# Loads of two batches issued from ScalarE's queue, and an instruction order from a table with a rank for every operation

## The chip, the cores and the metric

The kernel runs on one core of a Trainium2 chip. The core has TensorE (PE: matrix products, with its weight loads as PEld), VectorE (DVE), ScalarE (ACT), GpSimd (POOL) and SyncE (SP), which here only issues DMAs. The metric is the device time of one execution in microseconds; the median of the runs counts.

## The reference

Inputs are q, k and v of 4 batches, 8 heads, 576 positions and 64 features in float32, a memory `M_prev` (64 x 64 for each batch and head) with its norm `z_prev`, a gate `beta` for each head, and two weight matrices in float64 that the kernel reads as pairs of 32-bit words.

```python
scores = scale * np.matmul(q, k.transpose(0, 1, 3, 2))      # causal mask, softmax over the row
local = np.matmul(a, v)
q_p = phi(q)                                                # phi(x) = elu(x) + 1
mem_out = einsum('bhsd,bhde->bhse', q_p, M_prev) / mem_norm
attn = g * mem_out + (1 - g) * local
x = attn.transpose(0, 2, 1, 3).reshape(2304, 512)
h = x @ w_in                                                # 512 -> 2048
y = (np.maximum(h, 0) + alpha * np.minimum(h, 0)) @ w_out   # 2048 -> 512
```

## The kernel before

Precise products are made of float16 halves: a float32 value is split into a high and a low float16 part, and three of the four products are summed. Rows of the attention are worked off in blocks of 128: four blocks of 128 for each batch, and the first 64 rows of all four batches together as a fifth group (`Z`). For each batch `b`, `load_batch` (line 630) brings q, k, v, `M_prev` and `z_prev` into SBUF; keys go into tile `kn` and values into `vn`, of which there is one each, so that batch `b+1` can be loaded only when batch `b` has been read for the last time. `prep_qk`, `prep_v` and `prep_phi` (lines 825 to 904) find scales and the memory's norm; `build_qk` and `build_v` (lines 951 and 969) make the float16 halves and turn queries and keys by DMA transposes. For each head and pair of blocks, `unit_scores` makes the scores `s`, a VectorE operation masks them and finds the row's extreme, and ScalarE takes the exponential `E`. `unit_probs` (line 1056) writes the probabilities `P` as two halves (ScalarE the high, VectorE the low one) and has them turned by a DMA transpose into `PT`. `pair_values` (line 1096) multiplies `PT` with the values in the PSUM tile `bank`, splits the result into `xn` and has it turned by a DMA transpose into `x`. `moe_in` (line 1210) multiplies `x` with the first weights into `h`, and `moe_out` (line 1250) the activated `gg` with the second weights into `y`.

All DMAs, loads, stores and transposes alike, are issued from SyncE (`Y`); ScalarE is `A`. `load` (line 668) issues one load and gives its phase a name: `L2k`, for instance, is a load of batch 2's keys.

No engine's order is the order of the text. Every operation is first recorded by `Work.add` (line 282) with its dependences, its price (`price`, line 330) and its phase. `Work.issue` (line 459) then ranks the operations and calls `lay` (line 389), a list scheduler: each engine takes, when it is free, the ready operation of the lowest rank, by priced times. The operations are emitted in the order of the starts that `lay` gives. In the kernel before, the ranks come from a backward pass over the dependences, to which `STAGES` (line 32) adds biases by phase and by phase and engine, in two stages with further forward and backward passes. The phase names that the prediction uses are these: L2k to L3v are the loads of keys and values of batches 2 and 3, P21 is `unit_probs` of batch 2 for blocks 1 and 2, and `n` and `N` are warm-up products of TensorE on a tile of ones, at the start of the program, that nothing reads. The tile `stv` holds maxima of the values, from which scales are made.

Of the kernel before, what the change touches and what calls it, by code (L numbers as in the profile page):

```python
# [20 lines left out]
WC = [1, 1, 1, 1, 1, 1, 1, 1, 1, 1, 1, 1, 1, 1, 0, 1]  # L21
XB = 3
# [9 lines left out]
STAGES = [  # L32
    (2, {
        "A0": 10.6, "A:DVE": 50.6, "BK0": 102.5, "BK:ACT": -27.7, "BK:PE": 3.4, "C0": -56.4, "C1": 22.3, "C2": 335.8,
        "C3": -920, "C:ACT": 1096.2, "C:DVE": -3.8, "C:PE": -943.6, "I": -699.2, "I:DVE": 79.2, "I:POOL": 497.7,
        "J:ACT": 470.6, "J:DVE": 108, "J:PE": -179.3, "K": 47.5, "K:POOL": 2.3, "L0K": -713.8, "L0K:DMA": 228.2,
# [6 lines left out]
        "LW:DMA": 605.3, "LZ": 27.3, "LZ:DMA": -1145.9, "Lz": 8.5, "Lz:DMA": -8.6, "N": 87.9, "N:PE": 292.5,  # L43
        "P01": 4, "P03": 3.7, "P11": 777.2, "P13": 823.4, "P21": 168.1, "P23": 236.6, "P31": -675.3, "P33": -247.2,
        "P:ACT": 988.7, "P:DMA": 668.5, "P:DVE": -882.6, "P:PE": -157.8, "S0": 4737.2, "S1": -1253, "S3": -2953.6,
        "S:ACT": -87.5, "S:DVE": 168.1, "V0": -874.8, "V:DVE": 211.2, "V:PE": -90.8, "a0": 5.7, "a1": 46.8,
        "a2": -161.5, "a3": 389.6, "a4": -42.9, "a:ACT": -265.2, "a:DVE": 239.4, "bk0": -173.5, "bk1": 344.8,
        "bk2": 244.5, "bk3": 3.1, "bk:ACT": -687.5, "bk:DMA": 246.9, "bk:DVE": 1380.7, "bk:PE": 100.3, "bv0": -0.7,
# [5 lines left out]
        "o31": 144.8, "o33": 10.1, "o:ACT": -779.8, "o:DMA": 580.1, "o:DVE": -613.6, "o:PE": 33.3, "oZ": 10.8,  # L54
# [5 lines left out]
        "v:DVE": 634.9, "v:PE": 331.4, "x0": -121.5, "x:ACT": 2.1, "x:DVE": 73.7, "y0_10": -412.5, "y0_11": -68.6,  # L60
        "y0_30": 187.3, "y0_31": 1834.4, "y1_10": -18.1, "y1_11": 103.3, "y1_30": -419.6, "y1_31": 103.8,
        "y2_10": 184.2, "y2_11": 220.2, "y2_30": -3073.8, "y2_31": -122.6, "y3_10": 764.1, "y3_11": 98,
        "y3_31": 447.3, "y4_11": -1599.1, "y:ACT": -1231.1, "y:DMA": 642.8, "y:DVE": -750.7, "y:PE": 1282.7,
    }),
# [4 lines left out]
        "C3:PE": -8.9, "C:ACT": 13.2, "C:DVE": 9.3, "C:PE": -17.2, "I": -57.9, "I:POOL": -8.6, "J:ACT": -18.7,  # L69
# [6 lines left out]
        "LW3": -8.7, "LW3:DMA": -22.1, "LW:DMA": -2.8, "LZ:DMA": -42.6, "Lz:DMA": -4.4, "N": 0.9, "N:PE": -13.7,  # L76
# [5 lines left out]
        "P33:DMA": -3.8, "P33:DVE": -7.4, "P33:POOL": -37, "P:ACT": 15, "P:DMA": -20.1, "P:DVE": 8.9, "P:PE": -86.4,  # L82
# [126 lines left out]
        "y:PE": 143.8,  # L209
    }),  # L210
]
WINDOW = 3413.0
RING, SHARE = 1200, 0.95
NEG = -1.0e37
# [35 lines left out]
class Work:  # L250
# [31 lines left out]
    def add(self, kind, engine, name, a, kw):  # L282
# [35 lines left out]
        if kind == "DMA":  # L318
            hold, move, late, packets = hold
        elif kind == "PE":  # L320
            late = ins[0].shape[0] / 128
            x = kw.get("lhsT")
# [1205 lines left out]
```

## Time and profile before

| | us |
|---|---|
| three runs | 563.78, 561.42, 562.34 |
| median | 562.34 |
| profiled execution, device time | 563.66 |
| its span from the first to the last instruction | 561.9 |
| TensorE busy in the span | 536.4 |
| VectorE busy | 450.9 |
| ScalarE busy | 376.7 |

The profile is of one execution. The times of the runs are device times; the span leaves out what lies around the program's first and last instruction, 1.76 us here. A window row gives busy times of the engines in one stretch; TensorE's clock in it is the share of full speed that was granted. The DMA share in it adds up the times of the packets over the 16 DMA engines.

### The profile page before, as it was taken

The page shows a single profiled execution, that of the slowest core. Times are in us where ns is not written, and L with a number is a line of the kernel's source. Part 1 is how long each engine was busy: PE and PEld are TensorE (multiplying, and loading weights), DVE is VectorE, ACT ScalarE, POOL GpSimd, SP SyncE. Part 2 cuts the span into 40 slices and gives each one's busy share as a digit, 9 for nine tenths or more (in the row PEclk, how much of TensorE's full clock was granted, in tenths as well). Part 3 has the DMA queues.
Part 4 walks back from the last instruction along what each step waited for, and adds up shares of the span by engine and source line. Part 5 has one row for each costly group of instructions (what it writes and reads, how often), then busy time and mean ns, then how long its engine had stood idle before and what let it go on. Part 6 is the DMA issues. An engine that isn't in the chain of part 4 may idle for free. (4 is left out here: it accounts for less than half of the span.)

```text
span 561.9 us, 11984 instructions
## 1 busy us (share of the span) xinstructions
PE 536.4 (95%) x4421; PEld 353.5 (63%) x4421; DVE 450.9 (80%) x1197; ACT 376.7 (67%) x790; POOL 82.8 (15%) x142
## 2 busy tenths in 40 slices
PE   9749999999999899999998999999999999999997
PEld 3448654556557566658555766578578765866663
DVE  4989999999999799999897999998679974233232
ACT  2568996778998369978785787796579873232222
POOL 3000510031220012221222110431112110000000
PEclk9869999999999999999998999999999999999999
DMA  8998595836359997579999816799446963000000
GB/s 283 239 353 202 155 238 173 244 94 153 89 127 184 214 231 170 101 140 210 194 201 198 175 34 146 160 232 178 58 118 111 167 138 88 12 11 2 37 1 37
DMA packets 226026, 82.84 MB, mean 147 GB/s; under 512 B 216224, under 2 KB 216240, under 8 KB 225968
## 3 DMA queue, kind: packets, MB, share of 16 engines
q1 hardware_dynamic: 225968, 82.09, 64.5%
q8 instruction: 34, 0.56, 0.4%
q14 instruction: 24, 0.20, 0.1%
HBM read 35.66 MB, written 5.77 MB: 74 GB/s over the span
## 5 line engine op out<-in xcount | busy, mean ns | idle before, releaser
L487 PE MATMUL h<-x,R 128*128 128x256 f16 x1536 | 246.7, 273 | 1.9 <-DMA x<-xn 1.4
L487 PE MATMUL y<-R,gg 128*128 128x512 f16 (+1 forms) x832 | 247.0, 399 | 0.8 <-ACT k L487 0.6
L487 PE MATMUL bank<-v,PT 128*128 128x64 f16 x1224 | 182.1, 193 | 5.3 <-DMA PT<-P 4.5
L487 PEld LDWEIGHTS <-R 128*128 128x128 f16 x1536 | 148.6, 98 | 36.9 <-issue 6.5
L487 PEld LDWEIGHTS <-gg 128*128 128x128 f16 x768 | 74.4, 98 | 78.3 <-DVE gg L487 1.8
L487 PEld LDWEIGHTS <-PT 128*128 128x128 f16 x1224 | 114.4, 98 | 13.6 <-DMA PT<-P 6.9
L487 POOL TENSOR_SCALAR E<-q,nrm,sm 128x64 f32<-128x64 f32 x112 | 67.9, 618 | 310.9 <-DVE sm L487 269.8
L487 ACT ACTIVATE E<-E,mx 128x320 f32<-128x320 f32 (+3 forms) x136 | 81.1, 602 | 21.5 <-DVE mx L487 17.4
L487 DVE SCALAR_TENSOR_TENSOR P<-E,mx,P 128x384 f16<-128x384 f32 (+2 forms) x112 | 75.3, 699 | 8.5 <-ACT P L487 8.4
L487 ACT ACTIVATE P<-E,mx 128x384 f16<-128x384 f32 (+2 forms) x112 | 71.0, 675 | 15.8 <-POOL E L487 12.0
L487 DVE SCALAR_TENSOR_TENSOR r<-r,oma,h 128x256 f32<-128x256 f32 x128 | 56.6, 475 | 20.2 <-ACT r L487 20.0
L487 DVE SCALAR_TENSOR_TENSOR gg<-r,gsc,gg 128x512 f16<-128x512 f32 x56 | 41.8, 748 | 36.5 <-ACT gg L487 35.0
L487 ACT ACTIVATE r<-h 128x512 f32<-128x512 f32 x72 | 42.3, 589 | 35.8 <-PE h L487 23.9
L487 ACT ACTIVATE gg<-r,gsc 128x512 f16<-128x512 f32 x56 | 40.1, 717 | 37.4 <-PE y L487 33.4
L487 DVE CUSTOM_DVE_ANT_0 E<-s,mask,pm 128x320 f32<-128x320 f32 (+2 forms) x96 | 56.9, 608 | 7.6 <-PE s L487 7.5
L487 PE MATMUL s<-k,qT 128*128 128x64 f16 (+5 forms) x136 | 37.9, 294 | 1.3 <-DMA k<-k 1.3
L487 PE MATMUL s<-k,qS 128*128 128x192 f16 (+4 forms) x120 | 34.0, 294 | 0.0
L487 PE MATMUL h<-R 128*128 128x256 f32 x128 | 32.7, 383 | 0.0
L487 PEld LDWEIGHTS h<-R 128*128 128x128 f32 x128 | 22.3, 192 | 6.6 <-issue 3.0
L487 ACT ACTIVATION_READ_ACCUMULATOR E<-E,mx 128x1 f32 x124 | 23.5, 189 | 0.0
L487 ACT ACTIVATE xn<-bank,xsc 128x256 f16<-128x256 f32 x28 | 12.9, 462 | 12.3 <-PE bank L487 12.3
L487 DVE SCALAR_TENSOR_TENSOR xn<-bank,xsc,xn 128x256 f16<-128x256 f32 x28 | 13.4, 480 | 9.4 <-ACT xn L487 9.4
(183 smaller groups left out, 636.7 us busy)
## 6 DMA issues: line engine op xcount, KB each, us to landing
q<-in_q_dram SPq DMA_DIRECT2D x16, 256.0 KB, 4.3
vn<-in_v_dram SPq DMA_DIRECT2D x16, 256.0 KB, 5.2
out_dram<-t SPq DMA_DIRECT2D x16, 256.0 KB, 2.4
kn<-in_moe_w_in_dram SPq DMA_DIRECT2D x6, 512.0 KB, 6.7
kn<-in_moe_w_out_dram SPq DMA_DIRECT2D x6, 512.0 KB, 5.3
kn<-in_k_dram SPq DMA_DIRECT2D x12, 256.0 KB, 4.0
qS<-qT SPq DMA_DIRECT2D x24, 128.0 KB, 2.6
R<-in_moe_w_in_dram SPq DMA_DIRECT2D x4, 512.0 KB, 5.6
```

The source lines that it names most:

```text
L487: fn(*a, **kw)
```

## The change

Two things are changed. First, the loads of four phases, the keys and values of batches 2 and 3, are issued from ScalarE and no more from SyncE; `price`, `add` and `lay` learn that a DMA can be an operation of ScalarE. Secondly, `STAGES` with its backward passes is gone. In its place stands `PLAN`, a table with one rank for every operation of the program, 6253 in all, kept as differences under phase and engine; `issue` reads it and calls `lay` once. The prices of DMAs that `lay` uses are changed too. What is computed, the tiles and the operations remain as they are.

```diff
+ASIDE = ('L2k', 'L2v', 'L3k', 'L3v')
...
-STAGES = [
...
+PLAN = {
...
+    "L2k:ACT": "1959 -434 -66 47 1055",
+    "L2q:DMA": "1008 914 40 667 -99",
+    "L2v:ACT": "1575 63 -516 1340 -1369 1354",
+    "L3k:ACT": "3852 -400 -817 341 -99",
...
+    "L3v:ACT": "2938 -323 93 992 -880 1001",
...
+    "P21:ACT": "2836 -135 2 -585 610 -580 120 -122 633 -763 1082 288 -696 739 -700 197",
...
-        if kind == "DMA":
+        if kind == "DMA" or name == "dma_start":
             hold, move, late, packets = hold
...
-                return (800 + 1.75 * kb if kb > 400 else 1130 + 0.6 * kb), 190 + 3.45 * kb, 1655, -1
+                return (800 + 1.75 * kb, 4.1 * kb, 1700, -1) if kb > 400 else (1130 + 0.6 * kb, 3.78 * kb, 1885, -1)
...
-            return 620, (273 if kb > 200 else 200) + 4.17 * kb, 2100, packets
+            return (600, 4.5 * kb, 2050, packets) if kb > 200 else (620, 6 * kb, 2090, packets)
...
                 free[x] = done = t + hold
+                if x == "ACT" and move and not back:
+                    wire = max(wire, t + 100) + move
+                    done = wire + late
...
-        for passes, bias in STAGES:
-            rank = [x + 1e3 * sum(bias.get(k, 0) for k in dict.fromkeys((
-                op[7], op[7].rstrip("0123456789_") + ":" + op[0], op[7] + ":" + op[0]))) for x, op in zip(rank, ops)]
-            for n in range(passes):
-                if n:
-                    back = self.lay(after, before, [-s - h for s, h in zip(start, hold)], True)
-                    rank = [-s - h for s, h in zip(back, hold)]
-                start = self.lay(before, after, rank)
-            rank = start
+        plan = {}
+        for x, steps in PLAN.items():
+            at, ranks = 0, []
+            for step, _, times in (y.partition("*") for y in steps.split()):
+                for _ in range(int(times or 1)):
+                    at += int(step)
+                    ranks.append(100.0 * at)
+            plan[x] = iter(ranks)
+        start = self.lay(before, after, [next(plan[f"{op[7]}:{op[0]}"]) for op in ops])
...
     def load(o, i, phase):
         work.phase = phase
-        Y.dma_start(out=o, in_=i)
+        (A if phase in ASIDE else Y).dma_start(out=o, in_=i)
```

## Rows read from the trace of the kernel before

**Rows 1.** The page: busy time of the engines; the DMA queue.

```profile
PE 536.4 (95%) x4421; PEld 353.5 (63%) x4421; DVE 450.9 (80%) x1197; ACT 376.7 (67%) x790; POOL 82.8 (15%) x142
...
q1 hardware_dynamic: 225968, 82.09, 64.5%
```

**Rows 2.** Busy time by stretch: start:end and length, engines, clock, DMA share, GB/s.

```profile
20.00:44.00 24.00, 13.95 (x101) 10.77 (x102) 22.17 (x83) 15.49 (x52) 0.00 (x0) 0.66 1.12 291
180.00:196.00 16.00, 13.68 (x98) 8.86 (x95) 13.24 (x30) 6.74 (x11) 0.00 (x0) 1.00 0.98 200
280.00:292.00 12.00, 10.66 (x93) 5.96 (x92) 11.96 (x41) 10.09 (x23) 1.88 (x3) 1.00 1.16 225
292.00:304.00 12.00, 9.35 (x116) 7.46 (x114) 9.10 (x27) 7.77 (x19) 4.69 (x8) 1.00 1.01 174
304.00:308.00 4.00, 4.00 (x16) 1.71 (x14) 2.83 (x11) 2.04 (x5) 0.00 (x0) 0.57 0.93 210
...
196.00:212.00 16.00, 16.00 (x110) 10.43 (x108) 15.89 (x46) 11.65 (x29) 2.62 (x5) 1.00 1.02 230
212.00:240.00 28.00, 27.23 (x264) 18.85 (x262) 26.78 (x88) 25.52 (x58) 5.73 (x12) 1.00 0.63 138
460.00:558.00 98.00, 98.00 (x749) 63.51 (x745) 32.64 (x64) 30.20 (x48) 0.77 (x2) 1.00 0.10 28
...
304.00:320.00 16.00, 16.00 (x121) 11.26 (x119) 13.57 (x38) 10.38 (x25) 2.07 (x4) 0.89 1.03 217
```

**Rows 3.** TensorE's waits over the run: us in total, times, longest us.

```profile
PE bank L487 <- DMA PT<-P: 4.5, 5, 2.7
PE bank L487 <- DVE stv L487: 3.5, 1, 3.5
PE h L487 <- DVE P L487: 2.8, 1, 2.8
...
PE h L487 <- DMA x<-xn: 1.4, 2, 1.2
PE s L487 <- DMA k<-k: 1.3, 2, 0.9
```

**Rows 4.** SyncE's timeline: start us, us, what is issued.

```profile
198.58 4.04 SPq L487 DMA_DIRECT2D vn<-in_v_dram  x4
...
208.79 2.40 SPq L487 DMA_DIRECT2D kn<-in_k_dram  x2
...
294.14 2.07 SPq L487 DMA_DIRECT2D kn<-in_k_dram  x2
296.32 4.16 SPq L487 DMA_TRANSPOSE PT<-P  x1
...
300.59 1.33 SPq L487 DMA_TRANSPOSE PT<-P  x1
...
317.77 0.62 SPq L487 DMA_DIRECT2D kn<-in_k_dram  x1
```

**Rows 5.** VectorE's timeline from 292 us: the low halves of P.

```profile
292.70 1.06 DVE L487 SCALAR_TENSOR_TENSOR P<-E,mx,P 128x384 f16<-128x384 f32 x2 [0.47 <-ACT P L487]
...
294.68 1.01 DVE L487 SCALAR_TENSOR_TENSOR P<-E,mx,P 128x384 f16<-128x384 f32 x2
```

**Rows 6.** Timeline of all engines at 302 us: idle time before, releaser.

```profile
302.77 0.20 PE L487 MATMUL bank<-v,PT 128*128 128x64 f16 x1 [2.65 <-DMA PT<-P]
...
302.83 0.62 ACT L487 ACTIVATE P<-E,mx 128x384 f16<-128x384 f32 x1 [2.40 <-DMA PT<-P]
```

**Rows 7.** Tiles kn and PT, issues on SyncE: ns min/median/max, first and last start.

```profile
L487 SPq DMA_DIRECT2D kn<-in_k_dram x15: 399/868/2191, 124.2 to 317.8; - x15
...
L487 SPq DMA_TRANSPOSE PT<-P x56: 1309/1926/4159, 117.3 to 464.7; - x56
```

**Rows 8.** VectorE's timeline from 31 us: maxima of queries and of values.

```profile
31.51 0.68 DVE L487 TENSOR_REDUCE stq<-q 128x1 f32<-128x512 f32 x1
...
32.25 1.21 DVE L487 TENSOR_REDUCE stv<-R 128x1 f32<-128x1024 f32 x1
```

More of the change, by code (lines that the diff above doesn't have):

```diff
@@ L29 @@
 PN = [1, 1, 1, 1, 1]
-STAGES = [
[L33 to L36, printed above, removed]
[6 rows of a table removed]
[L43 to L48, printed above, removed]
[5 rows of a table removed]
-        "o31": 144.8, "o33": 10.1, "o:ACT": -779.8, "o:DMA": 580.1, "o:DVE": -613.6, "o:PE": 33.3, "oZ": 10.8,
[5 rows of a table removed]
[L60 to L64, printed above, removed]
[4 rows of a table removed]
-        "C3:PE": -8.9, "C:ACT": 13.2, "C:DVE": 9.3, "C:PE": -17.2, "I": -57.9, "I:POOL": -8.6, "J:ACT": -18.7,
[6 rows of a table removed]
-        "LW3": -8.7, "LW3:DMA": -22.1, "LW:DMA": -2.8, "LZ:DMA": -42.6, "Lz:DMA": -4.4, "N": 0.9, "N:PE": -13.7,
[5 rows of a table removed]
-        "P33:DMA": -3.8, "P33:DVE": -7.4, "P33:POOL": -37, "P:ACT": 15, "P:DMA": -20.1, "P:DVE": 8.9, "P:PE": -86.4,
[21 rows of a table removed]
-        "h4_11:PE": -16.7, "h:ACT": 10, "h:DVE": 8.9, "h:PE": -16.3, "n": -27.5, "n:PE": -9.4, "o01": -15,
[5 rows of a table removed]
-        "o33:DVE": 21.3, "o33:PE": -55.2, "o:ACT": -0.5, "o:DMA": -50.1, "o:DVE": 13.1, "o:PE": -18, "oZ": -97,
[4 rows of a table removed]
-        "q:ACT": 39, "q:DVE": 9.7, "r0:ACT": 0.9, "r0:DVE": 9.9, "r:ACT": 35.7, "r:DVE": 13.6, "s01:ACT": -1.2,
[4 rows of a table removed]
-        "s33:ACT": 1.7, "s33:PE": -49.1, "s:ACT": 12.1, "s:DVE": 8.9, "s:PE": -16.3, "sZ": 8.1, "sZ:ACT": 98.3,
[14 rows of a table removed]
-        "y4_11:PE": -16, "y:ACT": 21.9, "y:DMA": 2.5, "y:DVE": 8.4, "y:PE": -16.3,
-    }),
[4 rows of a table removed]
-        "C3:PE": -26.7, "C:ACT": 47.4, "C:DVE": -22.5, "C:PE": 1, "I:DVE": -32.9, "I:POOL": 4.3, "J": 37.8,
[13 rows of a table removed]
-        "P33:DMA": -13.2, "P33:DVE": -9.1, "P:DMA": -3.5, "P:DVE": -22.3, "P:PE": 0.2, "P:POOL": -11, "S0": 2.9,
[27 rows of a table removed]
-        "o33:PE": 65.8, "o:ACT": 7.4, "o:DMA": -10.7, "o:DVE": -24.8, "o:PE": 144.2, "oZ": -53.6, "oZ:ACT": 8.9,
[9 rows of a table removed]
-        "s33:DVE": -8.2, "s33:PE": 41.6, "s:ACT": -5, "s:DVE": -22.3, "s:PE": 143.8, "sZ": -0.9, "sZ:ACT": 37.5,
[15 rows of a table removed]
-        "y:PE": 143.8,
-    }),
-]
@@ L212 @@
+PLAN = {
[440 rows of a table added]
+}
 WINDOW = 3413.0
@@ L335, in price @@
         size = 2 if o.dtype == F16 else 4
-        if kind == "DMA":
+        if kind == "DMA" or name == "dma_start":
             kb = n * o.shape[0] * size / 1024
             if "transpose" in name:
-                return (800 + 1.75 * kb if kb > 400 else 1130 + 0.6 * kb), 190 + 3.45 * kb, 1655, -1
+                return (800 + 1.75 * kb, 4.1 * kb, 1700, -1) if kb > 400 else (1130 + 0.6 * kb, 3.78 * kb, 1885, -1)
             run = min(x.ap[-1][1] * (2 if x.dtype == F16 else 4) for x in (o, ins[0]))
@@ L342, in price @@
             if run < 256:
-                return 500, 0.45 * packets, 1800, packets
+                return 500, 0.45 * packets, 2000, packets
             if run >= 4096:
-                return 400, (2.75 if self.phase in ("LW0", "LW1") else 4.9) * kb, 2000, packets
+                rate, late = {"LW0": (3.2, 2600), "LW1": (2.7, 2450)}.get(self.phase, (3.55, 2150))
+                return 400, rate * kb, late, packets
             if run >= 512:
-                return 540, max(300, 4.06 * kb), 1800, packets
-            return 620, (273 if kb > 200 else 200) + 4.17 * kb, 2100, packets
+                if o.tensor.name in self.fixed:
+                    return 400, 1.4 * kb, 1950, packets
+                return (560, 5.3 * kb, 1765, packets) if kb < 200 else (530, 4 * kb, 1800, packets)
+            return (600, 4.5 * kb, 2050, packets) if kb > 200 else (620, 6 * kb, 2090, packets)
         if kind == "PE":
@@ L465, in issue @@
                 after[d].append((i, lag))
-        late = [0.0] * len(ops)
-        hold = [max(op[5], op[8][0]) for op in ops]
-        pe = 0.0
-        for i in reversed(range(len(ops))):
-            took = ops[i][8][0] + ops[i][8][1] if ops[i][0] == "DMA" else hold[i]
-            late[i] = min([late[f] - lag for f, lag in after[i]], default=0.0) - took
-            if ops[i][6]:
-                late[i] = pe = min(late[i], pe - hold[i])
-        rank = late
-        for passes, bias in STAGES:
-            rank = [x + 1e3 * sum(bias.get(k, 0) for k in dict.fromkeys((
-                op[7], op[7].rstrip("0123456789_") + ":" + op[0], op[7] + ":" + op[0]))) for x, op in zip(rank, ops)]
-            for n in range(passes):
-                if n:
-                    back = self.lay(after, before, [-s - h for s, h in zip(start, hold)], True)
-                    rank = [-s - h for s, h in zip(back, hold)]
-                start = self.lay(before, after, rank)
-            rank = start
+        plan = {}
[7 more added lines that the diff above has]
+        start = self.lay(before, after, [next(plan[f"{op[7]}:{op[0]}"]) for op in ops])
         with tc.manual_schedule():
```

581 rows, old and new, of tables (PLAN, STAGES) are left out of this document.

## The prediction

> **What bounds the kernel now.** I read the page's busy shares first [rows 1]: TensorE is busy 536.4 us of the 561.9 us span, VectorE 450.9, ScalarE 376.7. So the end hangs on TensorE; what counts is where TensorE isn't fed and where its clock is low. The stages show that [rows 2]. From 460 to 558 us TensorE is full (98.00 of 98.00) with VectorE at a third: the last fifth is a backlog of expert-layer products, and whatever is saved earlier comes off the end. From 20 to 44 us TensorE is busy for 13.95 of 24.00 us at a granted clock of 0.66; VectorE is then at 22.17 and the DMA share is 1.12, so the head runs on loads and on VectorE. Between them three stretches lose time: 180 to 196 (2.32 us idle), 280 to 292 (1.34) and 292 to 304 (2.65). After the last of these the granted clock is 0.57 over 304 to 308, a mix of the two levels, 1.2 and 2.4 GHz, with 86% at the lower. TensorE had stood idle for 2.65 us just before it.
>
> The list of TensorE's waits names the cause [rows 3]: in the head VectorE (stv 3.5 us, P 2.8), later transposed probabilities (PT<-P, 4.5 us in five waits), transposed x (1.4) and transposed keys (1.3). All three come by SyncE's queue, on which the loads stand too. So what TensorE waits for after the head comes by that queue, and the change is about that queue.
>
> **Loads leave SyncE's queue: the term that carries the forecast.** `load` now issues phases L2k, L2v, L3k and L3v from ScalarE: per batch five key loads, four full and one half value load and one load of M_prev, 11, so 22 in all. The queue at 292 to 304 us shows what they do there [rows 4]. Two key loads are issued from 294.14 on and take 2.07 us; the transpose PT<-P behind them is issued at 296.32 and holds the queue for 4.16 us, where the shortest of the 56 of its kind took 1.309 and the median 1.926 [rows 7]; the next one goes at 300.59. VectorE had written the probabilities of these two by 293.76 and 295.69 (292.70 + 1.06, 294.68 + 1.01) [rows 5]. They were issued 2.6 and 4.9 us after they could be. TensorE waits 2.65 us for the second, until 302.77 [rows 6]. Without the loads in front the second would land up to 4.9 us earlier, and the whole wait goes. With it goes the low clock behind it: 86% of 4.00 us at half speed lose 1.72 us. Together -4.4 us. What is late next is the P of the following unit, which ScalarE writes from 302.83 on and which itself waited 2.40 us for the same transpose [rows 6], so it moves forward as well. Batch 2's loads, issued from 198 to 211 us [rows 4], delay nothing on TensorE today (16.00 of 16.00 busy from 196 to 212 [rows 2]): 0.
>
> Here a rule speaks against the change. The trace has the DMA share at 0.93 to 1.16 from 280 to 320 us [rows 2], as high as in the head, so the transfers may be slow there by themselves. The Trainium skill, "DMA: Bandwidth & Descriptors", section "Issuing engines are not separate DMA queues", says that DMAs of all issuing engines run on the same 16 DMA engines and interleave, and that starting them from several engines saves only the sequencer's time to issue. The row of the 4.16 us issue agrees with half of that: what is lost is at the issue; whether it is lost there or only shows there, no row of before decides. It is the first rival.
>
> **Loads enter ScalarE's instruction stream.** Each issue will stand between two activations in ScalarE's list, which the trace shows executed one after the other. No row shows a DMA issued by ScalarE; the nearest are the same 22 loads on SyncE. Batch 2's eleven, from 198.58 to 211.19 us, took 11.41 us of SyncE's time, 1.04 each, batch 3's eleven, from 294.14 to 318.39, took 8.52, 0.77 each, and the last of these, with no load just before it, 0.62 [rows 4]; over all key loads the ends are 0.399 and 2.191 us [rows 7]. I take 0.77, the middle one, because ScalarE's queue starts empty but each batch's loads come close together: 11 x 0.77 = 8.5 us per batch. For batch 3 they lie beside idle time: from 292 to 320 ScalarE is idle for 28.00 - 7.77 - 10.38 = 9.85 us [rows 2]. For batch 2 they don't: from 196 to 212 it is idle for 16.00 - 11.65 = 4.35 us, and 4.1 us are pushed into 212 to 240, where it has 28.00 - 25.52 = 2.48 us left and VectorE is at 26.78 of 28.00 [rows 2]. Behind a held issue stand the exponentials and the P writes, and behind these VectorE, the next transpose and TensorE. The cost is between 0 (TensorE has expert-layer products to run meanwhile and is full from 196 to 212) and 4.1 us; nearer to 0 by that row, so +1.5. A gain is excluded for this edit alone: ScalarE gets work and loses none.
>
> **The order from a table.** The two staged passes go; every operation gets a rank of its own, and the list scheduler still lays them out by rank among what is ready. No operation is added or removed by that, so its price is in waits alone. After the load term, 2.32 + 1.34 = 3.7 us of idle time between 180 and 292 us can be won by a better place on SyncE's queue, or as much be lost by a worse one. I take half as a gain, -1.8: these waits are for transposes, and every transpose has 11 fewer neighbours per batch to be placed among. For the head I take 0. The warm-up products can't be moved into its gaps, since the scheduler gives TensorE whatever is ready, and before the first loads have landed nothing else is. Its bounds are -5 (the 3.5 us wait for stv and one low stretch like that at 304, 1.7 us) and +5. The products themselves cost the same in any order that keeps TensorE fed: 0, between -0.5 and +0.5.
>
> **The sum.** 561.9 - 4.4 + 1.5 - 1.8 = 557.2 us of span. The profiled execution took 563.66 us, 1.76 over its span, so 559.0; it is 1.3 above the median of the three runs, 562.34, so the forecast for the median is 562.34 - 4.7 = 557.6 us, 0.8% less. About 0.5%, or 2.8 us, is what a measurement of this kernel can tell from no change.
>
> **The rivals.**
>
> 1. The transfers are the limit, not their issue. With 82.09 MB on one queue at 64.5% of the engines' time [rows 1] and shares above 1 in just these stretches, the transposes move slowly beside the loads from whichever queue these come. Then the 2.65 us wait shrinks only by the issue time of the two loads, 2.07 us, the low stretch stays, ScalarE still costs 1.5: 562.34 - 2.1 + 1.5 = 561.7 us, no change. For it: the 4.16 us transpose holds the queue after both loads are issued. Against it: DMA share from 212 to 240 us is 0.63, so on the whole there is room.
>
> 2. ScalarE becomes the queue that stalls. All key loads of a batch become ready together, when the last reader of the one tile is done, and the table ranks most of them ahead of other work of that time (L2k 1459 to 2561, while P21's first operation on ScalarE has 2836). If both batches go at batch 2's pace, 11.41 us stand against 4.35 + 2.48 = 6.83 us of ScalarE's idle time from 196 to 240, and against 9.85 for batch 3: 4.6 + 1.6 us late, and a wait of such length brings one low stretch (1.7). 562.34 - 4.4 + 7.9 = 565.8 us, slower. It decides from 0.62 us per issue on (6.83 / 11). For it: ScalarE busy for 25.52 of 28.00 us there. Against it: TensorE's backlog, and a table laid out with those issues in it.
>
> 3. The head gets better too, by the 3.5 us wait and one low stretch: 557.6 - 5.2 = 552 us. For it: a maximum of batch 0 (0.68 us) runs on VectorE at 31.51, ahead of the stv maximum at 32.25 for which TensorE stands [rows 8]. Against it: all of the head is full of loads, DMA share 1.12.
>
> 4. The change doesn't do what it says: the transposes keep their late places and only the loads move. Then the wait stays and the time is that of before plus ScalarE's 1.5: about 564, within the no-change case.
>
> **How the numbers follow.** Forecast 0.47 (553 to 561), rivals 1 and 4 0.21 (560 to 565), rival 2 0.22 (564 to 570), rival 3 0.10 (549 to 553). The likeliest is 557.6. To hold 8 in 10 the range goes from the low bound of the sum (562.34 - 4.4 - 3.7 - 5 = 549) to rival 2's price, 566. Faster by over 0.5% (below 559.5): the forecast but for 0.04 at its upper end, and rival 3, 0.53. Within 0.5%: 0.21 + 0.04 + 0.03 of rival 2 = 0.28. Slower: 0.19.
>
> **What would show it.** Right: PT<-P issues on SyncE near 300 us at 1.3 to 2 us each, no wait of TensorE over 1 us there, full clock from 300 to 320 us, and ScalarE's load issues under 0.8 us. Rival 1: issues short but PT<-P landing as late as before. Rival 2: load issues on ScalarE over 1 us and waits of TensorE or VectorE for ScalarE between 200 and 240 us. Rival 3: a clock share over 0.66 from 20 to 44 us and TensorE busy for more than 13.95 us there. The prediction is wrong if the table opens waits where there are none now, between 60 and 180 or after 320 us, for which the trace of before gives no price.

## The result and the profile after

The changed kernel takes 568.38 us (median of four runs, 567.75 to 569.34), the kernel before, run beside it, 562.12 (four runs, 561.42 to 563.78): a ratio of 1.010, 95% interval 1.0074 to 1.0126. It is slower by 6 us, about 1%; forecast were 5 us less, and the range ended at 566. The profiled execution of after is the fastest of its four, 567.75 us with a span of 566.0, while that of before stands above its median, so the two traces differ by 4.1 us only (566.0 - 561.9).

The page of after, busy times and the DMA queues that carry the loads (packets, MB, share of 16 engines; compare [rows 1]):

```profile
PE 533.3 (94%) x4421; PEld 353.3 (62%) x4421; DVE 453.4 (80%) x1197; ACT 375.9 (66%) x790; POOL 80.1 (14%) x142
...
q1 hardware_dynamic: 206160, 77.11, 60.2%
q10 hardware_dynamic: 19808, 4.98, 4.2%
```

q10 is new: it is ScalarE's queue and carries 4.98 MB that q1 no longer has. The loads did move. The stretches of [rows 2] in after (start:end and length, engines, clock, DMA share, GB/s):

```profile
20.00:44.00 24.00, 12.00 (x98) 9.99 (x99) 20.78 (x93) 13.51 (x47) 0.00 (x0) 0.65 1.05 277
180.00:196.00 16.00, 15.51 (x132) 11.33 (x130) 16.00 (x36) 6.93 (x12) 0.00 (x0) 1.00 0.83 201
280.00:292.00 12.00, 10.21 (x110) 7.11 (x109) 10.79 (x33) 7.54 (x16) 0.76 (x2) 1.00 1.04 226
292.00:304.00 12.00, 10.50 (x91) 6.47 (x89) 8.92 (x27) 6.54 (x18) 3.29 (x6) 1.00 1.29 221
304.00:308.00 4.00, 3.48 (x45) 2.31 (x43) 3.86 (x11) 3.66 (x10) 0.00 (x0) 1.00 0.54 123
304.00:320.00 16.00, 14.56 (x151) 10.56 (x149) 14.24 (x51) 11.56 (x31) 2.83 (x6) 1.00 0.76 160
196.00:212.00 16.00, 15.32 (x108) 10.24 (x107) 14.78 (x43) 10.65 (x24) 2.69 (x4) 1.00 1.16 234
212.00:240.00 28.00, 26.91 (x252) 18.26 (x251) 26.94 (x85) 26.09 (x58) 5.83 (x12) 1.00 0.69 129
460.00:558.00 98.00, 98.00 (x794) 65.43 (x792) 37.99 (x78) 34.40 (x58) 1.90 (x4) 1.00 0.16 38
```

The places that the prediction looked at are better on the whole: 180 to 196 has 0.49 us of idle time in place of 2.32, 292 to 304 has 1.50 in place of 2.65, and from 304 to 308 us the clock is at full speed; only 280 to 292 is worse (1.79 in place of 1.34). The last 98 us are full, as before. So the loss lies where the prediction had not looked, and wider windows of both kernels find it. First before:

```profile
20.00:60.00 40.00, 29.68 (x239) 23.48 (x240) 37.70 (x114) 29.17 (x79) 0.00 (x0) 0.79 1.05 274
60.00:460.00 400.00, 390.01 (x3365) 258.54 (x3364) 368.47 (x996) 311.19 (x656) 77.74 (x127) 1.00 0.73 158
...
60.00:180.00 120.00, 118.33 (x783) 71.60 (x782) 116.66 (x306) 99.37 (x202) 23.65 (x33) 1.00 0.61 156
...
320.00:460.00 140.00, 139.41 (x1401) 97.42 (x1399) 123.98 (x341) 109.27 (x234) 28.30 (x50) 1.00 0.66 131
```

Then after:

```profile
20.00:60.00 40.00, 27.16 (x231) 22.40 (x232) 36.78 (x122) 26.69 (x72) 0.00 (x0) 0.79 1.02 258
60.00:460.00 400.00, 386.21 (x3311) 256.33 (x3311) 366.42 (x984) 307.81 (x652) 73.93 (x125) 1.00 0.73 157
...
60.00:180.00 120.00, 116.05 (x744) 69.05 (x744) 114.81 (x302) 99.34 (x206) 22.72 (x33) 1.00 0.62 160
...
320.00:460.00 140.00, 137.22 (x1343) 95.88 (x1342) 121.39 (x326) 107.78 (x230) 27.43 (x49) 1.00 0.65 130
```

From 60 to 460 us TensorE is busy for 3.80 us less, of which the low clock of before at 304 to 308 (1.72 us) is taken off: 2.1 us of work. More idle time stands from 60 to 180 us (3.95 us in place of 1.67) and from 320 to 460 (2.78 in place of 0.59), less between. From 20 to 60 us TensorE is busy for 2.52 us less; at the mean granted clock of 0.79 that is about 2.0 us of work at full speed. This is an estimate, since the low clock isn't spread evenly over the busy time: with every part at the clock granted in it, the stretch lacks 1.4 us, and the first 20 us another 0.9 (busy for 17.68 us in place of 18.57). Both ways head and rest lose about 2 us each, and the end shows the sum: from 460 us on TensorE, at full clock, is busy for 102.21 us in after and for 98.11 in before, 4.1 us more, the whole difference of the spans. TensorE's waits in after (us in total, times, longest; compare [rows 3]):

```profile
PE bank L747 <- DVE stv L747: 4.1, 1, 4.1
PE h L747 <- DVE P L747: 3.8, 1, 3.8
PE y L747 <- ACT gg L747: 3.0, 3, 1.5
PE bank L747 <- DVE xn L747: 2.5, 2, 2.0
PE y L747 <- DMA R<-in_k_dram: 1.9, 1, 1.9
...
PE s L747 <- DVE r L747: 1.8, 1, 1.8
...
PE bank L747 <- DMA PT<-P: 1.0, 2, 0.8
```

The waits for PT are down from 4.5 to 1.0 us. In their place stand waits for VectorE and ScalarE (gg, xn, r), none over 2.0 us, most of them between 160 and 420 us; there the waits for these two engines come to 8.6 us in place of 1.0. Both long waits of the head are longer (stv 3.5 to 4.1, P 2.8 to 3.8), and one for keys of group Z has grown from 0.3 to 1.9 us.

### The profile page after: what moved, and what is told of

Same layout as the page of the kernel before. It is cut to its first block, busy times and chain, and to the rows that moved or that the text cites. A ratio compares the mean times of both kernels' runs of the same rounds, so it can differ in the third digit from the quotient of the medians.

```text
span 566.0 us, 11957 instructions
## 1 busy us (share of the span) xinstructions
PE 533.3 (94%) x4421; PEld 353.3 (62%) x4421; DVE 453.4 (80%) x1197; ACT 375.9 (66%) x790; POOL 80.1 (14%) x142
## 3 DMA queue, kind: packets, MB, share of 16 engines
q10 hardware_dynamic: 19808, 4.98, 4.2%
## 5 line engine op out<-in xcount | busy, mean ns | idle before, releaser
L747 PE MATMUL h<-x,R 128*128 128x256 f16 x1536 | 250.3, 273 | 2.8 <-DMA x<-xn 1.8
L747 PE MATMUL bank<-v,PT 128*128 128x64 f16 x1224 | 168.7, 193 | 3.6 <-DVE xn L747 2.5
L747 PEld LDWEIGHTS <-PT 128*128 128x128 f16 x1224 | 108.0, 98 | 12.9 <-issue 7.7
L747 POOL TENSOR_SCALAR E<-q,nrm,sm 128x64 f32<-128x64 f32 x112 | 65.1, 593 | 320.8 <-DVE sm L747 250.2
L747 DVE SCALAR_TENSOR_TENSOR P<-E,mx,P 128x640 f16<-128x640 f32 (+3 forms) x112 | 76.0, 698 | 11.7 <-ACT P L747 11.1
L747 ACT ACTIVATE P<-E,mx 128x640 f16<-128x640 f32 (+3 forms) x112 | 71.3, 673 | 19.2 <-DMA PT<-P 8.9
L747 DVE CUSTOM_DVE_ANT_0 E<-s,mask,pm 128x576 f32<-128x576 f32 (+3 forms) x96 | 56.4, 609 | 3.3 <-PE s L747 3.0
L747 PE MATMUL s<-k,qT 128*128 128x448 f16 (+5 forms) x136 | 38.0, 294 | 2.7 <-DVE r L747 1.8
L747 ACT ACTIVATE R<-R,wsc 128x1024 f16<-128x1024 f32 x16 | 18.3, 1143 | 8.4 <-DVE R L747 8.4
```

The source lines that it names most:

```text
L747: fn(*a, **kw)
```

## The experiments

Two questions: what do the moved loads do, and what does the new order do? The theory was that the order alone makes the kernel slower; the rival was that ScalarE's load issues do. The changed kernel was not run again beside the later ones; each is told by its ratio to the kernel before, run beside it.

**Loads and order apart.** e1 is the kernel before, in its own order, with the 22 loads issued from ScalarE at the places that they have in that order; e2 is the changed kernel with the loads back on SyncE at their new places.

```diff
+ASIDE = ('L2k', 'L2v', 'L3k', 'L3v')
...
+    YA = work.Engine(work, "DMA", nc.scalar)
...
-        Y.dma_start(out=o, in_=i)
+        (YA if phase in ASIDE else Y).dma_start(out=o, in_=i)
```

```diff
+    AY = work.Engine(work, "ACT", nc.sync)
...
-        (A if phase in ASIDE else Y).dma_start(out=o, in_=i)
+        (AY if phase in ASIDE else Y).dma_start(out=o, in_=i)
```

> The order of before on every engine; only the 22 loads of L2k, L2v, L3k and L3v leave SyncE's list for ScalarE's, at the places where they stood in time. Theory A (the new order is what costs; the move of the loads is worth what was predicted, 4.4 us of stall near 300 us less 1.5 on ScalarE): 557 to 560 us, and no wait of TensorE for PT<-P over 1 us between 290 and 310 us. Rival B (the move itself costs, because ScalarE is held at the issues): 565 us or more, with load issues over 1 us on ScalarE and waits for ScalarE behind them. Rival C (the 16 DMA engines are the limit): 561 to 563 us, PT<-P as late as before.

> The new order on every engine, as the table lays it; only the 22 loads go back from ScalarE's list to SyncE's, at the places where they stand in time. Theory A (the order costs): 568 us or more, up to 572, since the relief of SyncE's queue is gone too. Rival B (ScalarE's issues cost): 562 to 565 us, and the waits of TensorE for ScalarE's gg near 295 us are gone.

Measured: e1 562.35 us, ratio to before 1.0001 [0.9983, 1.0018]; e2 567.77 us, 1.0104 [1.0081, 1.0127]. So the order by itself makes the whole of the loss, and the loads together are worth nothing that shows, in the one order or in the other.

e5 and e6 are e1 with one batch each (`ASIDE = ('L3k', 'L3v')` and `ASIDE = ('L2k', 'L2v')`).

> The order of before; only batch 3's eleven loads (L3k, L3v) leave SyncE's list for ScalarE's. Theory A1 (the move helps at batch 3, where a transpose waits behind loads, and costs at batch 2, where ScalarE is held; in the run that moved both, the two cancelled: +4.0 us of finished products from 280 to 320 us against -2.0 from 200 to 220): 559 to 560.5 us. Rival (the stall near 300 us of the kernel before belongs to single executions, not to the typical one): 561.5 to 562.5 us.

> The order of before; only batch 2's eleven loads (L2k, L2v) leave SyncE's list for ScalarE's. Theory A1: 564 to 565 us, with load issues of 1 to 2 us on ScalarE from 198 to 213 us and short waits of TensorE for scores and gg behind them. Rival: 562 us, no change.

Measured: batch 3 alone 561.18 us, 0.9979 [0.9963, 0.9995]; batch 2 alone 562.09 us, 0.9999 [0.9983, 1.0015]. So of the 4.4 us forecast for the loads batch 3's bring about 1.2 us (0.3 to 2.1) and batch 2's none that shows. e5 is faster than the kernel before, by little; that its gain is lost again when batch 2's loads move too (e1) isn't shown, since the intervals of e1 and e5 overlap. The trace of e5 shows the mechanism nonetheless, over 292 to 304, 304 to 308 and 60 to 460 us:

```profile
292.00:304.00 12.00, 11.20 (x129) 8.45 (x126) 10.30 (x31) 7.80 (x21) 4.22 (x5) 1.00 1.22 189
304.00:308.00 4.00, 2.65 (x30) 2.31 (x27) 3.52 (x12) 1.97 (x5) 0.77 (x2) 1.00 1.29 268
60.00:460.00 400.00, 391.25 (x3392) 259.85 (x3391) 368.72 (x992) 312.65 (x657) 79.20 (x129) 1.00 0.74 159
```

The wait and the low clock of before are gone; 1.35 us of idle time at 304 to 308 are new. The profiled execution of e5 (560.34 us) is 3.3 us below that of before (563.66), the median only 1.2 (561.18 against 562.4, which is 561.18 / 0.9979). A second profile of the kernel before was taken to see whether its wait at 300 us belongs to the one execution:

> The kernel before, unchanged, for a second profile. The first one's execution took 563.66 us, 1.5 over the median of 19 timed ones. If the 2.65 us wait at 300 us and the low clock behind it are in every execution, they are here again; if they belong to slow executions, this one, when nearer to 562, has a shorter wait there and full clock.

```profile
292.00:304.00 12.00, 8.97 (x110) 7.17 (x109) 8.96 (x26) 7.13 (x19) 4.05 (x6) 0.98 0.93 163
304.00:308.00 4.00, 4.00 (x16) 1.77 (x15) 2.34 (x10) 1.64 (x4) 0.00 (x0) 0.64 0.93 209
```

It is there again (3.03 us idle, clock 0.64), in an execution of 563.52 us. Both traces of before are above its medians, by 1 to 1.5 us. The executions that the median stands for left no trace, but two things on record tell of them. The mean granted clock of a whole execution of before is 0.981 or 0.982 in eleven of the 23 runs beside e5 (median 563.2 us) and 0.984 or more in the other twelve (561.6 us); both traced executions have 0.982, and the 1.72 us lost at 304 us are 0.003 of the span, just this difference. In e5 all twelve runs have 0.984 or more. And e6 still has batch 3's loads on SyncE: its traced execution, at 0.984, waits 1.51 us for PT at 302 us in place of 2.65, and the clock behind that wait stays full:

```profile
304.00:308.00 4.00, 4.00 (x37) 2.82 (x36) 3.44 (x11) 3.20 (x8) 0.34 (x1) 1.00 0.97 213
```

So the low clock at 304 us, and with it much of the 4.4 us, seems to belong to about half of the executions of before only. This is read from the clocks of runs without a trace, not seen in them.

**Where in the order the cost lies.** From here on the kernels have one fixed place for every operation, merged from the two orders as they were emitted. This is the edit of all of them; they differ in `ORDER`, and the loads of batches 2 and 3 are on ScalarE unless it is said otherwise.

```diff
+ORDER = (
...
+def places():
+    b = zlib.decompress(base64.b85decode(ORDER))
+    return [b[i] + 256 * b[i + 1] for i in range(0, len(b), 2)]
...
+        order = places()
...
-            for i in sorted(range(len(ops)), key=lambda i: (start[i], i)):
+            for i in order:
```

e3 has the new order for what starts in the scheduler's first 60 us and the old one behind it (loads on SyncE); e4 the old one first and the new one behind it; e9 is as e4 with the cut at 200 us.

> The new order for all operations that the scheduler starts in its first 60 us, the order of before for all the others; loads on SyncE. If the head of the new order costs what the two traces show by 60 us in finished products, 1.6 us: 563.7 us. If later waits absorb it: 562 us. If the head's effect is larger further on, since VectorE is behind: 565 us.

> The other half: the order of before for the first 60 us, the new order with the loads on ScalarE for the rest. If head and rest add up: 568.4 - 1.6 = 566.8 us. If most of the loss comes from the head by way of late work further on: 564 us or less.

> Order of the kernel before for everything that its scheduler starts in the first 200 us, order of the changed kernel behind it, loads of batches 2 and 3 on ScalarE. With the old order only for the first 60 us (e4) the time was 565.2 us. Theory A: the cost of the new order behind the head arises at 160 to 180 us, where TensorE finishes 16.1 us of products in place of 19.0 (72 products of two pairs into the one tile bank in a row, 2.2 us of waiting). Then this kernel comes out as the kernel before does, 562.0 to 562.8 us. Theory B: it arises behind 200 us, in many waits of about 1 us each. Then the time stays at 564.7 to 565.7 us. Half of each: about 563.7 us.

Measured: e3 564.64 us, 1.0047 [1.0027, 1.0067]; e4 565.21 us, 1.0066 [1.0044, 1.0088]; e9 570.04 us, 1.0164 [1.0138, 1.0191]. Head and rest both cost, and 0.47% and 0.66% add to 1.13%, about the loss of after; that leaves little for the cut itself at 60 us. The same split shows in TensorE's busy time (us), whatever else the kernels differ in:

| kernel | head | 20 to 60, clock | rest | 60 to 460 |
|---|---|---|---|---|
| before | old | 29.68, 0.79 | old | 390.01 |
| e1 | old | 29.77, 0.74 | old | 391.53 |
| e4 | old | 29.64, 0.74 | new | 387.25 |
| e3 | new | 27.00, 0.74 | old | 391.08 |
| e2 | new | 27.05, 0.79 | new | 386.91 |
| after | new | 27.16, 0.79 | new | 386.21 |

Three of the times of the rest hold 1.7 us without work, since a stretch with half the clock (1.2 in place of 2.4 GHz) lies in them: before (at 304 us), e3 (67) and e2 (283). Without them the old rests stand at 388.3 to 391.5 us and the new ones at 385.2 to 387.3, so the split holds, with about 1 us between the nearest two.

e9 sets a bound to this. It has more of the old order than e4 and is slower. TensorE's timeline shows a wait that neither parent has, so it comes with the cut (the granted clock behind it, from 218 to 222 us, is 0.57):

```profile
217.60 0.20 PE L429 MATMUL bank<-v,PT 128*128 128x64 f16 x1 [3.49 <-DMA PT<-P]
```

So an order can't be cut up at will, and the cost behind the head can't be laid to 60 to 200 us or to what follows by such a cut.

**The head.** In after the three loads of `z_prev` and the one of alpha stand on SyncE between queries and keys, and the last keys of group Z are issued at 21.2 us in place of 18.8. e8 puts these four loads earlier on SyncE's list; e10 gives SyncE the old list for the first 60 us and leaves the other engines theirs.

> The new order, loads on ScalarE as the change has them; only four small loads at the start (three of z_prev, one of alpha) go back ahead of the first queries in SyncE's list, about where the order of before has them; in the new order they stand ahead of the last keys of the first group. If these late keys are why the head of the new order is behind: 566.5 us. If not: 568.4 us.

> The changed kernel with one edit: SyncE's list of DMAs within the scheduler's first 60 us stands in the order of the kernel before, the lists of the other engines in the new one. Theory A: the head's cost (about 2.5 us) comes from the order of loads on SyncE's queue, the last keys of group Z being issued at 21.2 us in place of 18.8. Then 565.5 to 566.3 us. Theory B: it comes from the order of VectorE and ScalarE in the head, to which the loads no more than conform. Then 568 us, as the changed kernel, or more, since these lists were laid out for the other order of loads (moving four loads alone, in e8, took 1.3 us more).

Measured: e8 569.72 us, 1.0135 [1.0109, 1.0162]; e10 570.16 us, 1.0165 [1.0141, 1.0189]. Neither is faster than after (1.010), e10 is slower, and from 20 to 60 us TensorE is busy for less than in after (27.16): 26.01 us in e8, 24.78 in e10. The wait for the keys does shrink (to 1.0 us in two pieces, in both kernels), but behind it stands a longer one for VectorE than in after, where it took 0.2 us; e8:

```profile
27.58 0.34 PE L429 MATMUL bank<-ident,ast 128*1 128x128 f32 x1 [3.10 <-DVE ast L429]
```

In e10 the same wait takes 2.65 us. So putting back SyncE's list, in part or whole, doesn't by itself win back the head.

**Waits behind the head.** The longest new wait of TensorE between 60 and 280 us is for xn. Its timeline in after at 175 us:

```profile
174.90 1.33 PE L747 MATMUL bank<-v,PT 128*128 128x64 f16 x40
178.23 1.09 PE L747 MATMUL bank<-v,PT 128*128 128x64 f16 x32 [2.00 <-DVE xn L747]
```

and VectorE's, in the same execution:

```profile
172.32 1.40 DVE L747 SCALAR_TENSOR_TENSOR q<-q,scr,q 128x512 f16<-128x512 f32 x2
173.64 1.28 DVE L747 SCALAR_TENSOR_TENSOR q<-q,t 128x512 f32<-128x512 f32 x2
174.85 1.28 DVE L747 TENSOR_TENSOR t<-q,zb 128x512 f32<-128x512 f32 x2
...
177.70 0.47 DVE L747 SCALAR_TENSOR_TENSOR xn<-bank,xsc,xn 128x256 f16<-128x256 f32 x1
```

72 products into the one tile `bank` follow each other, 40 of one pair and 32 of the next, and the second pair must wait until the first has been read; VectorE meanwhile prepares the queries of the next batch. e11 puts 20 products of the expert layer between the two pairs; e12 does the like at five more waits.

> The changed kernel with one edit in TensorE's list alone: 20 products of the expert layer (h<-x,R), which stand behind the 72 products of two pairs into the tile bank, are put between the two pairs, where TensorE waits 2.00 us for VectorE's second half of xn at 178.23 us. All other engines keep their lists. Theory A: the new order costs what its single waits of TensorE cost, each in full, since TensorE bounds the kernel. Then 20 x 0.11 = 2.2 us of work fill the wait and the time falls by 2.0, to 566.4 us (from 568.4). Theory B: TensorE's waits only show where it runs ahead of VectorE and ScalarE; a filled wait comes back as another one before the last fifth. Then 568.4 us, within 0.7.

> As the run before, and five further waits of TensorE are filled in the same way, each with products from behind it that belong to another block: those at 170.14 us (0.97 us, ten products), 282.44 (1.79, ten), 296.87 (1.50, fifteen), 318.02 (0.92, two of 0.22) and 366.07 (0.95, ten). Sum of the waits that can be filled: 2.0 + 0.97 + 1.79 + 1.50 + 0.44 + 0.95 = 7.7 us. Theory A: each wait costs itself, so 560.7 us, and with half of it filled in fact about 564.5. Theory B: the waits return elsewhere, 567.5 to 569 us.

Measured: e11 570.09 us, 1.0138 [1.0107, 1.0170]; e12 569.77 us, 1.0139 [1.0108, 1.0169]. Theory A falls. In e11 the inserted products wait themselves, and longer:

```profile
174.77 1.33 PE L429 MATMUL bank<-v,PT 128*128 128x64 f16 x40
179.08 3.33 PE L429 MATMUL h<-x,R 128*128 128x256 f16 x15 [2.99 <-DVE r L429]
```

They need `h`, which VectorE reads (r) behind the same preparation. The wait isn't TensorE's own; it was VectorE's list that set it. And behind this longer wait the granted clock falls, which it does nowhere from 60 to 460 us in after:

```profile
179.00:183.00 4.00, 3.92 (x23) 2.81 (x23) 4.00 (x9) 2.49 (x4) 0.00 (x0) 0.57 0.83 184
```

A second wait of 2.43 us, for gg at 299 us, is followed by 0.66 from 298 to 303 us. About 1.7 us of what e11 lost is low clock, at each of the two. The next theory was that VectorE and ScalarE take single operations too late. e13 is e11 with the operations that read TensorE's results put ahead of the preparation on both engines from 165 to 183 us; e14 does this from 60 to 460 us with the six waits filled, e16 from 130 to 460 without filling; e15 and e17 do it to the old order with batch 3's loads alone on ScalarE (e5), from 60 and from 130 us.

> The filled wait of e11 came back on VectorE: the 20 products waited 2.99 us for VectorE's r, which stands behind eight operations of the next batch's preparation (172.32 to 177.31 us) although its input was there by about 172.3. This run is e11 with the lists of VectorE and ScalarE changed between 165 and 183 us only: operations that read TensorE's results (five of VectorE's, three of ScalarE's) go ahead of the preparation behind which they stand, VectorE's half of xn goes one place ahead; nothing else moves. Theory A: the order's cost sits in such placements, and curing this one brings what TensorE waited there, 2.0 us against the changed kernel and 3.0 against e11: 566.4 us. Theory B: what is pushed back (2.6 us of preparation) is late for the next scores, and the time stays at 568 to 570 us.

> The changed kernel with the six waits of e12 filled and, over 60 to 460 us, all 47 operations of VectorE and ScalarE that read TensorE's results put ahead of the preparation behind which they stood by over 0.5 us after their input was there. Theory A (placement of single operations on VectorE and ScalarE behind preparation is the order's cost behind the head): TensorE's idle time from 60 to 460 us falls from 13.8 us towards the 10.0 of the kernel before, 564 to 565 us. Theory B (the order's cost lies in how the attention chain and the preparation share VectorE as a whole; each place cured opens another): 567 to 570 us.

> The same rule on the order of the kernel before, with batch 3's loads alone on ScalarE (e5, 561.2 us): 62 operations that read TensorE's results go ahead of preparation. Theory A of e14 gives a gain here too, since TensorE stands idle for 10.0 us from 60 to 460: 558 to 560 us. Theory B: 561 us, or slower where the preparation pushed back is late, 562 to 565 us.

> The changed kernel, with TensorE's list as it is, and with the 20 operations of VectorE and ScalarE from 130 to 460 us that read TensorE's results ahead of the preparation behind which they stood. The moves from 60 to 130 us of e14, which brought waits of up to 8.8 us at 100 to 120 us, are left out. Theory A (single late placements): up to 3 us less than the changed kernel, 565.5 us. Theory B (the arrangement as a whole): 567.5 to 570 us.

> The same rule from 130 to 460 us on the order of the kernel before with batch 3's loads on ScalarE (e5, 561.2 us), 25 operations moved. Theory A: 558.5 to 560 us. Theory B: 560.5 to 563 us.

Measured: e13 568.73 us, 1.0142 [1.0110, 1.0173]; e14 590.86 us, 1.0539 [1.0510, 1.0569]; e15 584.30 us, 1.0419 [1.0390, 1.0449]; e16 570.18 us, 1.0136 [1.0109, 1.0163]; e17 561.66 us, 0.9996 [0.9976, 1.0016]. In e13 the inserted products still wait 2.39 us for r. In e14 and e15 the loss is at 80 to 160 us, where operations were moved by more than 10 us and engines stood in front of them; TensorE's timeline of e14:

```profile
115.55 0.59 PE L429 MATMUL bank<-wsq,ones 128*128 128x4 f32 x2 [8.84 <-ACT kn L429]
```

They tell only that these moves were wrong. e16 and e17 are without them and bring nothing: in e16 TensorE's busy time from 60 to 460 us is no higher than in after (386.21).

```profile
60.00:460.00 400.00, 384.90 (x3294) 255.00 (x3293) 365.94 (x979) 305.37 (x647) 73.04 (x125) 1.00 0.72 156
```

What follows: behind the head the cost is spread over many waits of 0.5 to 2 us, and the moves that were tried at some of them won nothing. No single placement that was tried holds it. That it belongs to the arrangement as a whole is what is left over, not a mechanism that was shown.

## Why the prediction was wrong

**What bounds the kernel.** Right. The last fifth is full in both kernels, and what is lost earlier shows at the end: about 2 us of TensorE's work up to 60 us and 2.1 from there to 460 make the 4.1 us between the traces.

**The load term, -4.4 us: mis-sized.** What it said of 300 us came true in part: no wait over 1 us for PT there, full clock from 300 to 320 us, but other waits over 1 us (1.35 us for x in e5, 1.50 for gg in after). It is worth 1.2 us for batch 3 alone and nothing that shows for both batches. Two errors are in it. The whole wait of one profiled execution, with the low clock behind it, was counted as a gain of the median, although that execution stood 1.3 us above the median and, by their granted clocks, only about half of the executions seem to have the low clock; and the transposes were to be short once the loads had left the queue. They are not. The issues of PT from 286 to 320 us on SyncE (ns min/median/max, first and last start) in before, where the loads share the queue:

```profile
L487 SPq DMA_TRANSPOSE PT<-P x7: 1316/1887/4159, 283.8 to 314.8; - x7
```

in e5, where they are on ScalarE's:

```profile
L488 SPq DMA_TRANSPOSE PT<-P x7: 1279/2472/3855, 282.7 to 312.0; - x7
```

and in after:

```profile
L747 SPq DMA_TRANSPOSE PT<-P x7: 1332/1507/3982, 286.7 to 319.2; - x7
```

A transpose still holds SyncE's queue for close to 4 us. That is the half of rival 1 that [rows 4] left undecided: the time shows at the issue, whichever queue the loads come by. The Trainium skill's "DMA: Bandwidth & Descriptors", section "Issuing engines are not separate DMA queues", says that starting DMAs from several engines saves only the sequencer's time. e1, where 22 loads change the issuing engine and the time stays (1.0001), agrees.

**ScalarE's issues, +1.5 us: the issue time was right, the cost doesn't show.** Sum of the eleven issues of batch 2 in after: 6.87 us, of batch 3: 11.31, so 18.2 where 17 were expected. The 1.5 us were for batch 2, and e6, which moves these alone, is between 1.0 us faster and 0.8 us slower than before. Rival 2's place was wrong: it is batch 3 whose issues are long, and "they lie beside idle time" failed for it. ScalarE and TensorE at 290 us in after:

```profile
288.96 2.06 ACTq L747 DMA_DIRECT2D kn<-in_k_dram  x1
...
291.06 3.04 ACTq L747 DMA_DIRECT2D kn<-in_k_dram  x1
...
294.20 0.45 ACT L747 ACTIVATE E<-E,mx 128x192 f32<-128x192 f32 x1 [4.68 <-issue]
```

```profile
296.87 0.39 PE L747 MATMUL y<-R,gg 128*128 128x512 f16 x1 [1.50 <-ACT gg L747]
```

Two loads keep ScalarE for 5.1 us, and 1.50 us of TensorE's waiting for gg follow. But with the loads on SyncE (e2) the kernel is as slow; there another wait takes the place.

**The order from a table, -1.8 us with the head at 0: the step that failed.** It costs 5.8 us (e2, 1.04% of 562.2). The step looked at the two stretches with idle time and asked whether a new order would win or lose there; there after wins 1.4 us (2.28 us of idle time in place of 3.66), about the 1.8 that were forecast. But an order that ranks all 6253 operations anew has no reason to keep the other stretches as good as they were. The step also took over that what TensorE waits for behind the head comes by SyncE's queue; that held for the old order, while in after 8.6 us of the waits from 160 to 420 us are for VectorE and ScalarE. "The products themselves cost the same in any order that keeps TensorE fed" was right, and whether TensorE stays fed was the question. The prediction named this case in its last sentence (waits where there are none now, between 60 and 180 or after 320 us), and it came: the idle time grew by 2.3 us in the one stretch and by 2.2 in the other. But the prediction gave it no price, no chance and no rival; the range ended at rival 2.

**The head, 0 within -5 and +5.** It costs about 2 us by the traces and 2.6 by e3, within the bounds. Rival 3 had the sign wrong: the maximum of batch 0's queries does stand behind that of the values now, but so do both maxima of the values behind fourteen operations on group Z's scores (30.19 to 32.38 us). In the kernel before the first of these maxima ran ahead of the scores:

```profile
27.17 1.21 DVE L487 TENSOR_REDUCE stv<-R 128x1 f32<-128x1024 f32 x1
```

Only the second was left for 32.25 [rows 8]; in after both follow each other and take 2.34 us where one took 1.21, and TensorE's wait for stv ends at 35.13 us in place of 34.32:

```profile
32.23 0.22 DVE L747 CUSTOM_DVE_ANT_0 P<-s,mz 128x64 f32<-128x64 f32 x1
...
32.38 2.34 DVE L747 TENSOR_REDUCE stv<-R 128x1 f32<-128x1024 f32 x2
```

**Still open.** What in the new order costs the rest of the head's 2 us, beside the 0.8 us by which stv is late and the late keys, and what costs the 2 us or more behind it. Spreading the 72 products evenly over their neighbourhood, as against e11's one insertion, contradicts the lists of the other engines and wasn't tried.

## What to carry to other kernels

A new order of a full kernel is a change of every stretch, so its price has two sides even where nothing is added: before a gain at the visible waits is counted, there has to be a case in which the stretches without waits get worse. A wait seen in one execution that stands above the median is not yet a wait of the median: the granted clocks of the other runs can tell how many of them share it. And when a filled wait comes back on another engine, that engine's list set it; curing single waits in a list laid out as a whole brought nothing here (e11 to e17).

## What was not expected of the hardware

A load of keys issued from ScalarE took 0.37 to 3.04 us of ScalarE's own time, so an engine that computes can be held by its queue as SyncE is. And a lower clock need not cost anything. TensorE's granted clock from 20 to 60 us was 0.79 in two executions of the kernel before and in e5, but 0.74 in e1 with the same order of the head. First before, then e1, where the two differ most:

```profile
31.00:34.40 3.40, 0.08 (x1) 0.08 (x1) 3.40 (x22) 3.40 (x16) 0.00 (x0) 1.00 1.02 391
```

```profile
31.00:34.40 3.40, 0.37 (x1) 0.08 (x1) 3.37 (x17) 3.40 (x14) 0.00 (x0) 0.50 0.98 349
```

TensorE waits for stv there, so the half clock of e1 falls on time in which it had next to nothing to do.
